# Loading four key heads at a time: 32 partitions per head, one 16 KB row per partition, weights turned on VectorE

## The chip, the cores and the metric

The kernel runs on 1 core of one Trainium2 chip. The metric is the time of one execution on the device, in microseconds (us); the kernel before takes 199.07 us (median of 3 runs, 198.92 to 199.16). A run that is more than 1.5% above the fastest of its kernel counts as slow and is left out of comparisons.

Words used below, as they apply to this kernel: TensorE does the matrix products and writes them to PSUM; VectorE and ScalarE copy from PSUM and do the work between the products; SyncE issues the loads. A *packet* is one record of the DMA in the trace, a run of contiguous bytes (8 KB of keys or values in the kernel before). The profile counts 16 DMA engines for the core. A *unit* is the work for 4 key heads of one batch entry; there are 16 units.

## The reference, cut to what matters

One decoding step: 8 batch entries with one token each, 16 query heads, 8 key heads of size 256, and only the last 1,024 of 4,096 cached positions. The result is mixed with a small MLP.

```python
# x (8, 1, 448); k_cache, v_cache (8, 8, 4096, 256), bf16; W = 1024; rep = 2
q = (x @ wq).reshape(B, 1, 16, 256).transpose(0, 2, 1, 3)
k = repeat(k_cache[:, :, Sk - W:, :], 2, axis=1)
v = repeat(v_cache[:, :, Sk - W:, :], 2, axis=1)
scores = einsum("bhqd,bhkd->bhqk", q, k) * 256 ** -0.5
p = softmax(scores)
a = einsum("bhqk,bhkd->bhqd", p, v)...reshape(B, 1, 4096) @ wo
out = g * a + (1 - g) * mlp(layernorm(x))      # g: a sigmoid gate per token
```

The keys and values that are needed are 8 x 8 x 1,024 x 256 x 2 bytes, twice: 67.1 MB. In memory, the 1,024 rows of one head are one contiguous block of 512 KB; the blocks of two heads lie 2 MB apart.

## The kernel before

A ring of 18 buffers of 1 MB is filled by loads from SyncE in the order of use. One load brings 2 heads; partition p holds 16 rows (8 KB) of one head. The pattern on the memory side `s a (c d)` names the 64 row groups first and the 2 heads second, so heads alternate from partition to partition.

```python
QUAD = 4; GP = 2; NCK = 16; SK = 64; SLOT = 4096; RING = 18      # cut

def kv_loader(src, b, g):
    def load(t):
        nc.sync.dma_start(
            t[:],
            src[b, g : g + GP, kv_base:Sk, :].rearrange(
                "a (s c) d -> s a (c d)", c=NCK
            ),
        )
    return load
```

In each unit TensorE turns the keys in 64 blocks of 128x128, VectorE and ScalarE copy them from PSUM, TensorE makes the scores, and the softmax follows. Because the heads alternate over the partitions, ScalarE writes every exponential twice; 16 matmuls then turn the weights, and VectorE multiplies the wrong head's half with zero.

```python
def scores(u):                                   # cut
    nc.tensor.matmul(                            # 2 columns of weights, every 2nd column of keys
        S_ps[32 * a : 32 * a + rep, hf * NMM : (hf + 1) * NMM],
        lhsT=qw[:, j, b, h0 : h0 + rep],
        rhs=KT[a // GP][:, j, hf * CMM : (hf + 1) * CMM, :, a % GP], ...)

def softmax(u):                                  # cut
    nc.vector.reduce_max(nmx[:], S_ps[:], axis=AXIS.X, negate=True)
    nc.scalar.activation(                        # 1,024 scores to 2,048 exponentials
        E[:].rearrange("p (k a) -> p k a", a=GP),
        S_ps[:].rearrange("p (k o) -> p k o", o=1).to_broadcast([P, W, GP]),
        ACT.Exp, bias=nmx[:], scale=1.0, accum_out=rowsum[:])

def weights(u):                                  # cut
    for c in range(NCK):                         # 16 matmuls turn the weights
        nc.tensor.matmul(sm[:, c, :], lhsT=E[:, c * P : (c + 1) * P], rhs=sel[:], ...)
    nc.vector.tensor_tensor(ET[:], sm[:, 0:NCK, :], own[:]..., op=ALU.mult)

for u in range(1, NQ - 2):                       # the order of a unit
    transpose_keys(u)
    values(u - 1, *weights(u - 1))
    scores(u)
    softmax(u)
```

Of the kernel before, what the change touches and what calls it, by code (L numbers as in the profile page):

```python
# [17 lines left out]
def kernel(  # L18
# [38 lines left out]
    GP = 2  # L57
    NCK = NC * GP
    SK = P // GP
    SLOT = 4096  # L60
# [4 lines left out]
    RING = 18  # L65
    NMM = 512
    CMM = NMM // SK
# [30 lines left out]
    def kv_loader(src, b, g):  # L98
        def load(t):
            nc.sync.dma_start(  # L100
                t[:],
                src[b, g : g + GP, kv_base:Sk, :].rearrange(
                    "a (s c) d -> s a (c d)", c=NCK
                ),
            )

        return load
# [22 lines left out]
    def add_kv(name, src, u):  # L130
        b, half = divmod(u, Hkv // QUAD)
        for s in range(2):
            add((name, u, s), kv_loader(src, b, half * QUAD + 2 * s))

    wq_m = A_wq[0:DM, :].rearrange("(p r) n -> p r n", r=NR)
# [5 lines left out]
    W2A = SLOT // D  # L141

    add_kv("k", A_k_cache, 0)
    add(("w1", 0), rows_loader([w1_m[:, 0 : 2 * F]]))
    add(("w1", 1), rows_loader([w1_m[:, 2 * F : 3 * F], w1_t]))
    for r in range(NR):
        add(("wq", r), rows_loader([wq_m[:, r, :]]))
    add(("wq", NR), rows_loader([wq_t]))
    add(("w2", 0), rows_loader([w2_v[:, 0 : W2A * D]]))
    add(("w2", 1), rows_loader([w2_v[:, W2A * D : NF * D]]))  # L150
# [7 lines left out]
    for q in range(NHQ):  # L158
        for j0, j1 in WO_PARTS[q]:
            add(("wo", q, j0), rows_loader([wo_v[:, q, j0 * D : j1 * D]]))  # L160

    def slot(*key):
        return slots[index[key]]
# [36 lines left out]
    sel = consts.tile([P, RQ], BF16)  # L200
    qw = consts.tile([P, NJ, NB, Hq], BF16)
# [18 lines left out]
    for h in range(2):  # L220
        nc.vector.tensor_copy(xz[:, h, h::2], x_sb[:, DM:D])
    transposed(xT, x_sb, xz)
    nc.vector.tensor_copy(
        sel[:].rearrange("p (a i) -> p a i", i=rep),
        ident[:].rearrange("p (a s) -> p a s", a=QUAD)[:, :, 0:rep],
    )

    par = consts.tile([P, GP], F32)
    own = consts.tile([P, RQ], F32)
    nc.vector.reduce_sum(  # L230
        par[:], ident[:].rearrange("p (s a) -> p a s", a=GP), axis=AXIS.X
    )
    nc.vector.tensor_copy(
        own[:].rearrange("p (t a i) -> p t a i", a=GP, i=rep),
        par[:]
        .rearrange("p (t a i) -> p t a i", t=1, i=1)
        .to_broadcast([P, QUAD // GP, GP, rep]),
    )
# [61 lines left out]
    def transpose_keys(u):  # L300
        for s in range(2):
            kn = slot("k", u, s)
            kt = ktpool.tile([P, NJ, NCK, SK, GP], BF16, tag="kt", name="kt")
            KT[s] = kt
            ktf = kt[:].rearrange("p j c s a -> p j (c s a)")
            for c0 in range(0, NCK, NC):
                for j in range(NJ):
                    ktp = ps_kt.tile([P, W], BF16, tag="ktp", name="ktp")
                    for c in range(NC):
                        o = (c0 + c) * Dh + j * P  # L310
                        nc.tensor.transpose(  # L311
                            ktp[:, c * P : (c + 1) * P], kn[:, o : o + P], ident[:]
                        )
                    dst = ktf[:, j, c0 * P : (c0 + NC) * P]
                    if evac[0] % 8 in (2, 4, 7):
                        nc.scalar.copy(dst, ktp[:])  # L316
                    else:
                        nc.vector.tensor_copy(dst, ktp[:])  # L318
                    evac[0] += 1
            done()  # L320

    def query():
        qt = ps_misc.tile([P, Hq * NJ, NB], F32, tag="misc", name="qt")
        for r in range(NR + 1):
            w = slot("wq", r)
            for k in range(Hq * NJ):
# [4 lines left out]
                    lhsT=w[:, c : c + P],  # L331
# [5 lines left out]
            done()  # L337
        for j in range(NJ):
            nc.vector.tensor_scalar_mul(  # L339
                qw[:, j, :, :],  # L340
                qt[:].rearrange("p (h j) b -> p j b h", j=NJ)[:, j],
                qscale,
            )

    def scores(u):
        b, half = divmod(u, Hkv // QUAD)
        for hf in range(W // NMM):
            for j in range(NJ):
                for a in range(QUAD):
                    h0 = (half * QUAD + a) * rep  # L350
                    nc.tensor.matmul(  # L351
                        S_ps[32 * a : 32 * a + rep, hf * NMM : (hf + 1) * NMM],
                        lhsT=qw[:, j, b, h0 : h0 + rep],
                        rhs=KT[a // GP][:, j, hf * CMM : (hf + 1) * CMM, :, a % GP],
# [6 lines left out]
    def softmax(u):  # L361
        nmx = epool.tile([P, 1], F32, tag="nmx", name="nmx")
        nc.vector.reduce_max(nmx[:], S_ps[:], axis=AXIS.X, negate=True)  # L363
        E = epool.tile([P, W * GP], BF16, tag="E", name="E")
        rowsum = epool.tile([P, 1], F32, tag="rowsum", name="rowsum")
        nc.scalar.activation(  # L366
            E[:].rearrange("p (k a) -> p k a", a=GP),
            S_ps[:].rearrange("p (k o) -> p k o", o=1).to_broadcast([P, W, GP]),
            ACT.Exp,
            bias=nmx[:],  # L370
            scale=1.0,
            accum_out=rowsum[:],
# [3 lines left out]
    def weights(u):  # L376
        E, rowsum = soft.pop(u)
        rsum = epool.tile([P, 1], F32, tag="rsum", name="rsum")
        nc.vector.reciprocal(rsum[:], rowsum[:])
        selr = epool.tile([P, RQ], F32, tag="selr", name="selr")  # L380
        nc.vector.tensor_scalar(  # L381
            selr[:], sel[:], rsum[:], float(GP), op0=ALU.mult, op1=ALU.mult
        )
        sm = ps_sm.tile([P, NCK + 1, RQ], F32, tag="sm", name="sm")
        for c in range(NCK):
# [207 lines left out]
```

## Time and profile before

| | before | where it is read |
|---|---|---|
| time | 199.07 us | runs |
| TensorE, VectorE, ScalarE busy | 75%, 48%, 42% | part 1 of the page |
| bytes read | 77.68 MB | part 3 |
| rate from 30 to 180 us | 417 GB/s | windows |
| row maximum to row maximum | 10.16 us in most units, 10.24 in the mean of 12 | times of the row maxima, 39.40 to 49.56 and 39.40 to 162.27 us |
| last output-weight piece lands | 193.44 us | chain of waits |

From the page of the kernel before: the span in 40 slices of 4.9 us. A digit is a tenth: for PEclk of the full TensorE clock, for DMA of the mean busy time of the 16 engines. Then the hardware queue (packets, MB, share of all 16 engines' time), the shares of the chain that ended last, and the loads (times issued, KB, us from issue to landing).

```profile
PEclk9996556999999996799999999999999999997555
DMA  4999999999999999999999999999999999999960
GB/s 170 416 427 406 420 412 414 421 414 424 411 414 419 419 419 416 414 419 419 423 411 411 423 416 423 409 418 423 416 416 413 418 419 419 421 411 416 413 246 23
...
q1 hardware_dynamic: 11424, 77.68, 95.8%
...
DMA 49%; PE 26%; DVE 16%; ACT 5%; issue 2%; SPq 0%; ACTq 0%
...
slot<-in_A_k_cache_dram SPq DMA_DIRECT2D x32, 1024.0 KB, 19.9
slot<-in_A_v_cache_dram SPq DMA_DIRECT2D x32, 1024.0 KB, 19.9
```

The DMA engines hardly rest between the start and the end (9 tenths or more in slices 2 to 38): loads set the time. The groups of instructions (line, engine, operation, shapes, count, then busy us and mean ns of one) show the parts that the change touches. `slot` is a buffer of the ring, `ktp` the turned keys in PSUM, `kt` their copy, `S_ps` the scores, `nmx` the row maximum, `E` the exponentials, `sm` and `ET` the turned weights, `po` the attention's outputs:

```profile
L311 PE MATMUL ktp<-ident,slot 128*128 128x128 bf16 x1024 | 73.9, 232 | 21.6 <-ACT kt L316 15.2
...
L366 ACT ACTIVATE E<-S_ps,nmx 128x2048 bf16<-128x2048 f32 x16 | 31.5, 1968 | 72.2 <-DVE nmx L363 72.2
...
L351 PE MATMUL S_ps<-kt,qw 128*2 128x512 bf16 x256 | 18.1, 402 | 0.4 <-DVE qw L339 0.4
...
L386 PE MATMUL sm<-sel,E 128*128 128x8 bf16 x256 | 8.8, 167 | 1.7 <-ACT E L366 1.7
```

The last column is the idle time just before, and what ended most of it. The key transposes waited 15.2 us in all for ScalarE's copies, which stand behind the exponential of 1.97 us.

### The profile page before, as it was taken

What the parts mean: (1) busy time and instruction counts of PE and PEld (TensorE: products, weight loads), DVE (VectorE), ACT (ScalarE), POOL (GpSimd) and SP (SyncE); (2) the same over time, 40 slices, a digit from 0 to 9 for tenths busy, and PEclk for the clock granted to TensorE, in tenths of its full rate; (3) what the DMA queues carried; (4) which work ended last, traced back from release to release, by engine and by line L of the source; (5) the groups of instructions that cost most, each with busy time, mean ns of one, the idle gap of its engine ahead of it and who ended that gap; (6) DMA issues with size and microseconds to landing.
All of it is one profiled execution on the core that took longest, in us unless ns stands there. A gap on an engine that the chain in (4) does not pass through costs nothing.

```text
span 197.0 us, 6578 instructions
## 1 busy us (share of the span) xinstructions
PE 147.7 (75%) x3006; PEld 125.1 (64%) x3006; DVE 94.3 (48%) x230; ACT 82.0 (42%) x85; POOL 0.9 (0%) x7
## 2 busy tenths in 40 slices
PE   1699869868686878979596868686868686887662
PEld 0699739656574758877575667575656665675641
DVE  6540335364646464555545454636363636763200
ACT  3250043272636354362718180808172727383000
POOL 1000000000000000000000000000000000000000
PEclk9996556999999996799999999999999999997555
DMA  4999999999999999999999999999999999999960
GB/s 170 416 427 406 420 412 414 421 414 424 411 414 419 419 419 416 414 419 419 423 411 411 423 416 423 409 418 423 416 416 413 418 419 419 421 411 416 413 246 23
DMA packets 11645, 78.10 MB, mean 396 GB/s; under 512 B 1489, under 2 KB 1890, under 8 KB 3042
## 3 DMA queue, kind: packets, MB, share of 16 engines
q1 hardware_dynamic: 11424, 77.68, 95.8%
q8 instruction: 23, 0.38, 0.8%
q10 hardware_dynamic: 194, 0.02, 0.1%
q14 instruction: 4, 0.03, 0.0%
HBM read 77.68 MB, written 0.01 MB: 394 GB/s over the span
## 4 chain that ended last, share of the span: by engine, by line
DMA 49%; PE 26%; DVE 16%; ACT 5%; issue 2%; SPq 0%; ACTq 0%
DMA slot<-in_A_v_cache_dram 31%; PE ktp L311 10%; DMA slot<-in_A_wq_dram 8%; DVE kt L318 7%; PE po L414 7%; DMA slot<-in_A_wo_dram 7%; DVE nmx L363 6%; PE S_ps L351 5%; ACT kt L316 4%; DMA slot<-in_A_k_cache_dram 3%; PE sm L393 2%; ACT E L366 1%; DVE ET L395 1%; DVE selr L381 1%; PE bb L484 1%
## 5 line engine op out<-in xcount | busy, mean ns | idle before, releaser
L311 PE MATMUL ktp<-ident,slot 128*128 128x128 bf16 x1024 | 73.9, 232 | 21.6 <-ACT kt L316 15.2
L311 PEld LDWEIGHTS <-slot 128*128 128x128 bf16 x1024 | 66.1, 105 | 33.3 <-issue 28.3
L318 DVE COPY kt<-ktp 128x1024 bf16<-128x1024 bf16 x80 | 52.5, 686 | 30.3 <-PE ktp L311 29.0
L366 ACT ACTIVATE E<-S_ps,nmx 128x2048 bf16<-128x2048 f32 x16 | 31.5, 1968 | 72.2 <-DVE nmx L363 72.2
L316 ACT COPY kt<-ktp 128x1024 bf16<-128x1024 bf16 x48 | 47.1, 1013 | 19.3 <-PE ktp L311 19.3
L414 PEld LDWEIGHTS <-slot 128*128 128x128 bf16 x1024 | 29.5, 99 | 6.8 <-issue 6.8
L414 PE MATMUL po<-ET,slot 128*128 128x4 bf16 x1024 | 28.1, 164 | 5.3 <-DVE ET L395 5.3
L363 DVE TENSOR_REDUCE nmx<-S_ps 128x1 f32<-128x1024 f32 x16 | 19.6, 1225 | 13.0 <-PE S_ps L351 13.0
L351 PE MATMUL S_ps<-kt,qw 128*2 128x512 bf16 x256 | 18.1, 402 | 0.4 <-DVE qw L339 0.4
L423 DVE TENSOR_TENSOR oT<-po,rb 128x8 bf16<-128x8 f32 x32 | 4.3, 190 | 26.5 <-PE po L414 26.5
L393 PE MATMUL sm<-selr,ones_f 128*128 128x8 f32 x32 | 6.6, 279 | 5.5 <-DVE selr L381 5.5
L386 PE MATMUL sm<-sel,E 128*128 128x8 bf16 x256 | 8.8, 167 | 1.7 <-ACT E L366 1.7
L393 PEld LDWEIGHTS sm<-selr,ones_f 128*128 128x128 f32 x32 | 5.2, 203 | 6.8 <-DVE selr L381 6.6
L386 PEld LDWEIGHTS <-E 128*128 128x128 bf16 x256 | 8.2, 97 | 1.8 <-ACT E L366 1.8
L395 DVE TENSOR_TENSOR ET<-sm,own 128x128 bf16<-128x128 f32 x16 | 4.7, 291 | 8.2 <-PE sm L393 8.2
L351 PEld LDWEIGHTS <-qw 128*2 128x2 bf16 x256 | 4.7, 82 | 5.2 <-DVE qw L339 0.5
L545 PE MATMUL A_ps<-slot,oP 128*8 128x112 bf16 x128 | 4.3, 290 | 2.8 <-DMA slot<-in_A_wo_dram 2.1
L545 PEld LDWEIGHTS <-oP 128*8 128x8 bf16 x128 | 2.9, 113 | 4.1 <-issue 3.4
L329 PE MATMUL qt<-xT,slot 128*128 128x8 bf16 x128 | 3.9, 168 | 0.8 <-DMA slot<-in_A_wq_dram 0.4
L329 PEld LDWEIGHTS <-slot 128*128 128x128 bf16 x128 | 3.7, 104 | 1.0 <-DMA slot<-in_A_wq_dram 0.6
L381 DVE TENSOR_SCALAR selr<-sel,rsum 128x8 f32<-128x8 bf16 x16 | 3.7, 231 | 0.6
L552 DVE SCALAR_TENSOR_TENSOR res<-A_ps,gg_s,mixb 128x112 bf16<-128x112 f32 x1 | 0.3, 335 | 6.6 <-PE A_ps L545 6.6
(69 smaller groups left out, 38.9 us busy)
## 6 DMA issues: line engine op xcount, KB each, us to landing
slot<-in_A_k_cache_dram SPq DMA_DIRECT2D x32, 1024.0 KB, 19.9
slot<-in_A_v_cache_dram SPq DMA_DIRECT2D x32, 1024.0 KB, 19.9
slot<-in_A_wq_dram SPq DMA_DIRECT2D x3, 1024.0 KB
slot<-in_A_wo_dram SPq DMA_DIRECT2D x3, 896.0 KB, 19.1
slot<-in_B_w_dram SPq DMA_DIRECT2D x1, 1008.0 KB
slot<-in_B_w_dram SPq DMA_DIRECT2D x1, 896.0 KB
slot<-in_B_w_dram SPq DMA_DIRECT2D x1, 560.0 KB
slot<-in_A_wq_dram SPq DMA_DIRECT2D x1, 512.0 KB
```

Of the source, the lines that this page charges most:

```text
L311: nc.tensor.transpose(ktp[:, c * P : (c + 1) * P], kn[:, o : o + P], ident[:])
L316: nc.scalar.copy(dst, ktp[:])
L318: nc.vector.tensor_copy(dst, ktp[:])
L329: nc.tensor.matmul(qt[:, k, :], lhsT=w[:, c : c + P], rhs=xT[:, r + half, :], start=(r == 0 and k == 0), stop=(r == NR), skip_group_check= ...
L351: nc.tensor.matmul(S_ps[32 * a : 32 * a + rep, hf * NMM : (hf + 1) * NMM], lhsT=qw[:, j, b, h0 : h0 + rep], rhs=KT[a // GP][:, j, hf * CMM ...
L363: nc.vector.reduce_max(nmx[:], S_ps[:], axis=AXIS.X, negate=True)
L366: nc.scalar.activation(E[:].rearrange("p (k a) -> p k a", a=GP), S_ps[:].rearrange("p (k o) -> p k o", o=1).to_broadcast([P, W, GP]), ACT.Exp,
L386: nc.tensor.matmul(sm[:, c, :], lhsT=E[:, c * P : (c + 1) * P], rhs=sel[:], start=True, stop=True,)
L393: nc.tensor.matmul(sm[:, NCK, :], lhsT=ones_f[:], rhs=selr[:], start=True, stop=True)
L395: nc.vector.tensor_tensor(ET[:], sm[:, 0:NCK, :], own[:].rearrange("p (o r) -> p o r", o=1).to_broadcast([P, NCK, RQ]), op=ALU.mult,)
L414: nc.tensor.matmul(PO[:, j, cols], lhsT=vn[:, o : (c + 1) * Dh : NJ], rhs=ET[:, c, cols], start=(c == 0), stop=(c == NCK - 1),)
L545: nc.tensor.matmul(dst, lhsT=oP[:, j, q, :], rhs=w[:, o + cols.start : o + cols.stop], start=(q == 0 and j == 0), stop=(q == NHQ - 1 and j ...
```

## The change

The intent: longer runs for the DMA engines (16 KB instead of 8 KB), one load for four heads, and less compute. Each head gets its own 32 partitions. The exponentials are then needed once only, and a VectorE transpose, which the program counts on to turn blocks of 32x32, puts the weights where the values need them. The weights that TensorE holds for the scores are 8 columns wide, 6 of them zero; the rows of foreign heads get a maximum so low that their exponentials are zero. The diff, cut to its core:

```diff
-    NCK = NC * GP          # 16
-    SK = P // GP           # 64
-    SLOT = 4096
-    RING = 18
+    SK = P // QUAD         # 32
+    NCK = W // SK          # 32
+    SLOT = 8192
+    RING = 9
@@ loads @@
-    def kv_loader(src, b, g):
-        def load(t):
-            nc.sync.dma_start(
-                t[:],
-                src[b, g : g + GP, kv_base:Sk, :].rearrange(
-                    "a (s c) d -> s a (c d)", c=NCK
-                ),
-            )
+    def kv_loader(src, u, parts):
+        b, half = divmod(u, Hkv // QUAD)
+        v = src[b, half * QUAD : (half + 1) * QUAD, kv_base:Sk, :].rearrange(
+            "a (s c) d -> a s (c d)", c=NCK
+        )
+        def load(t):
+            n = NCK * Dh // parts
+            for i in range(parts):
+                nc.sync.dma_start(
+                    t[:, i * n : (i + 1) * n], v[:, :, i * n : (i + 1) * n]
+                )
@@ scores @@
-                        S_ps[32 * a : 32 * a + rep, hf * NMM : (hf + 1) * NMM],
-                        lhsT=qw[:, j, b, h0 : h0 + rep],
-                        rhs=KT[a // GP][:, j, hf * CMM : (hf + 1) * CMM, :, a % GP],
+                        S_ps[32 * a : 32 * a + RQ, hf * CH * SK : (hf + 1) * CH * SK],
+                        lhsT=qw[:, j, b, half, a, :],
+                        rhs=KT[hf][:, j, :, a * SK : (a + 1) * SK],
@@ softmax and weights @@
+        nc.vector.tensor_tensor(nmx[:], nmx[:], cap[:], op=ALU.min)
-            E[:].rearrange("p (k a) -> p k a", a=GP),
-            S_ps[:].rearrange("p (k o) -> p k o", o=1).to_broadcast([P, W, GP]),
-            ACT.Exp, ...
+            E[:], S_ps[:], ACT.Exp, bias=nmx[:], scale=1.0, accum_out=rowsum[:]
-        for c in range(NCK):
-            nc.tensor.matmul(sm[:, c, :], lhsT=E[:, c * P : (c + 1) * P], rhs=sel[:], ...)
-        nc.vector.tensor_tensor(ET[:], sm[:, 0:NCK, :], own[:]..., op=ALU.mult)
+        nc.vector.transpose(ET[:].rearrange("p c r -> p (c r)"), E[:])
[... value loads and weight loads: one buffer where there were two; the rest is bookkeeping ...]
```

In the loader, `s a` has become `a s`: the memory side now names the 4 heads first, which gives each head its own 32 partitions.

More of the change, by code (lines that the diff above doesn't have):

```diff
@@ L56 @@
     NQ = NB * Hkv // QUAD
-    GP = 2
-    NCK = NC * GP
-    SK = P // GP
-    SLOT = 4096
+    SK = P // QUAD
+    NCK = W // SK
+    NH = 2
+    CH = NCK // NH
+    SLOT = 8192
     HPQ = 4
@@ L64 @@
     WO_PARTS = [[(0, NJ8)]] * (NHQ - 1) + [[(0, 4), (4, 6), (6, 8)]]
-    RING = 18
-    NMM = 512
-    CMM = NMM // SK
+    RING = 9
+    BIG = 1e30
     qscale = float(Dh) ** -0.5
@@ L128, in add, with add_kv @@
         plan.append(loader)
-    def add_kv(name, src, u):
-        b, half = divmod(u, Hkv // QUAD)
-        for s in range(2):
-            add((name, u, s), kv_loader(src, b, half * QUAD + 2 * s))
-    wq_m = A_wq[0:DM, :].rearrange("(p r) n -> p r n", r=NR)
+    def add_kv(name, src, u, parts=1):
+        add((name, u), kv_loader(src, u, parts))
+    wq_m = A_wq[0:DM, :].rearrange("(p r) n -> p (r n)", r=NR)
     wq_t = A_wq[DM:D, :].rearrange("r (h n) -> (r h) n", h=2)
@@ L140 @@
     wo_v = A_wo.rearrange("(q p j) n -> p q (j n)", p=P, j=NJ8)
-    W2A = SLOT // D
-    add_kv("k", A_k_cache, 0)
-    add(("w1", 0), rows_loader([w1_m[:, 0 : 2 * F]]))
-    add(("w1", 1), rows_loader([w1_m[:, 2 * F : 3 * F], w1_t]))
-    for r in range(NR):
-        add(("wq", r), rows_loader([wq_m[:, r, :]]))
-    add(("wq", NR), rows_loader([wq_t]))
-    add(("w2", 0), rows_loader([w2_v[:, 0 : W2A * D]]))
-    add(("w2", 1), rows_loader([w2_v[:, W2A * D : NF * D]]))
+    add_kv("k", A_k_cache, 0, parts=2)
+    add(("w1",), rows_loader([w1_m, w1_t]))
+    add(("wq", 0), rows_loader([wq_m[:, 0 : 2 * HD]]))
+    add(("wq", 1), rows_loader([wq_m[:, 2 * HD : 3 * HD], wq_t]))
+    add(("w2",), rows_loader([w2_v]))
     for u in range(1, NQ - 1):
@@ L157 @@
         add_kv("v", A_v_cache, u)
-    for q in range(NHQ):
-        for j0, j1 in WO_PARTS[q]:
-            add(("wo", q, j0), rows_loader([wo_v[:, q, j0 * D : j1 * D]]))
+    for q in range(0, NHQ, 2):
+        add(
+            ("wo", q),
+            rows_loader(
+                [
+                    wo_v[:, q + i, j0 * D : j1 * D]
+                    for i in range(2)
+                    for j0, j1 in WO_PARTS[q + i]
+                ]
+            ),
+        )
     def slot(*key):
@@ L199 @@
     yT = consts.tile([P, NX, NB], BF16)
-    sel = consts.tile([P, RQ], BF16)
-    qw = consts.tile([P, NJ, NB, Hq], BF16)
+    sel = consts.tile([P, RQ], F32)
+    qw = consts.tile([P, NJ, NB, Hq // RQ, QUAD, RQ], BF16)
     oT = consts.tile([P, Hq, NJ, NB], BF16)
@@ L222 @@
     transposed(xT, x_sb, xz)
-    nc.vector.tensor_copy(
-        sel[:].rearrange("p (a i) -> p a i", i=rep),
-        ident[:].rearrange("p (a s) -> p a s", a=QUAD)[:, :, 0:rep],
-    )
-    par = consts.tile([P, GP], F32)
-    own = consts.tile([P, RQ], F32)
-    nc.vector.reduce_sum(
-        par[:], ident[:].rearrange("p (s a) -> p a s", a=GP), axis=AXIS.X
-    )
-    nc.vector.tensor_copy(
-        own[:].rearrange("p (t a i) -> p t a i", a=GP, i=rep),
-        par[:]
-        .rearrange("p (t a i) -> p t a i", t=1, i=1)
-        .to_broadcast([P, QUAD // GP, GP, rep]),
-    )
+    nc.vector.reduce_sum(
+        sel[:], ident[:].rearrange("p (a s) -> p s a", a=QUAD)[:, 0:RQ, :], axis=AXIS.X
+    )
+    cap = consts.tile([P, 1], F32)
+    rows = consts.tile([P, 1], F32)
+    for a in range(QUAD):
+        nc.vector.reduce_sum(
+            rows[32 * a : 32 * a + 32, :],
+            ident[32 * a : 32 * a + 32, (32 + rep) * a : (32 + rep) * a + rep],
+            axis=AXIS.X,
+        )
+    nc.vector.tensor_scalar(
+        cap[:], rows[:], 2.0 * BIG, -BIG, op0=ALU.mult, op1=ALU.add
+    )
+    nc.vector.memset(qw[:], 0.0)
     def norm_and_gate():
@@ L300, in transpose_keys @@
     def transpose_keys(u):
-        for s in range(2):
-            kn = slot("k", u, s)
-            kt = ktpool.tile([P, NJ, NCK, SK, GP], BF16, tag="kt", name="kt")
-            KT[s] = kt
-            ktf = kt[:].rearrange("p j c s a -> p j (c s a)")
-            for c0 in range(0, NCK, NC):
+        kn = slot("k", u)
+        for hf in range(NH):
+            kt = ktpool.tile([P, NJ, CH, P], BF16, tag="kt", name="kt")
+            KT[hf] = kt
+            for c0 in range(0, CH, NC):
                 for j in range(NJ):
-                    ktp = ps_kt.tile([P, W], BF16, tag="ktp", name="ktp")
+                    ktp = ps_kt.tile([P, NC, P], BF16, tag="ktp", name="ktp")
                     for c in range(NC):
-                        o = (c0 + c) * Dh + j * P
-                        nc.tensor.transpose(
-                            ktp[:, c * P : (c + 1) * P], kn[:, o : o + P], ident[:]
-                        )
-                    dst = ktf[:, j, c0 * P : (c0 + NC) * P]
+                        o = (hf * CH + c0 + c) * Dh + j * P
+                        nc.tensor.transpose(ktp[:, c, :], kn[:, o : o + P], ident[:])
+                    dst = kt[:, j, c0 : c0 + NC, :]
                     if evac[0] % 8 in (2, 4, 7):
@@ L319, in transpose_keys @@
                     evac[0] += 1
-            done()
+        done()
     def query():
@@ L324, in query @@
         for r in range(NR + 1):
-            w = slot("wq", r)
+            w, o = slot("wq", r // 2), (r % 2) * HD
             for k in range(Hq * NJ):
@@ L330, in query @@
                     qt[:, k, :],
-                    lhsT=w[:, c : c + P],
+                    lhsT=w[:, o + c : o + c + P],
                     rhs=xT[:, r + half, :],
@@ L336, in query @@
                 )
-            done()
-        for j in range(NJ):
-            nc.vector.tensor_scalar_mul(
-                qw[:, j, :, :],
-                qt[:].rearrange("p (h j) b -> p j b h", j=NJ)[:, j],
-                qscale,
-            )
+        done(2)
+        qv = qt[:].rearrange("p (g a i j) b -> p a j b g i", g=Hq // RQ, a=QUAD, i=rep)
+        for a in range(QUAD):
+            for j in range(NJ):
+                nc.vector.tensor_scalar_mul(
+                    qw[:, j, :, :, a, a * rep : (a + 1) * rep], qv[:, a, j], qscale
+                )
     def scores(u):
         b, half = divmod(u, Hkv // QUAD)
-        for hf in range(W // NMM):
+        for hf in range(NH):
             for j in range(NJ):
                 for a in range(QUAD):
-                    h0 = (half * QUAD + a) * rep
                     nc.tensor.matmul(
-                        S_ps[32 * a : 32 * a + rep, hf * NMM : (hf + 1) * NMM],
-                        lhsT=qw[:, j, b, h0 : h0 + rep],
-                        rhs=KT[a // GP][:, j, hf * CMM : (hf + 1) * CMM, :, a % GP],
+                        S_ps[32 * a : 32 * a + RQ, hf * CH * SK : (hf + 1) * CH * SK],
+                        lhsT=qw[:, j, b, half, a, :],
+                        rhs=KT[hf][:, j, :, a * SK : (a + 1) * SK],
                         start=(j == 0),
@@ L363, in softmax @@
         nc.vector.reduce_max(nmx[:], S_ps[:], axis=AXIS.X, negate=True)
-        E = epool.tile([P, W * GP], BF16, tag="E", name="E")
+        nc.vector.tensor_tensor(nmx[:], nmx[:], cap[:], op=ALU.min)
+        E = epool.tile([P, W], BF16, tag="E", name="E")
         rowsum = epool.tile([P, 1], F32, tag="rowsum", name="rowsum")
         nc.scalar.activation(
-            E[:].rearrange("p (k a) -> p k a", a=GP),
-            S_ps[:].rearrange("p (k o) -> p k o", o=1).to_broadcast([P, W, GP]),
-            ACT.Exp,
-            bias=nmx[:],
-            scale=1.0,
-            accum_out=rowsum[:],
+            E[:], S_ps[:], ACT.Exp, bias=nmx[:], scale=1.0, accum_out=rowsum[:]
         )
@@ L377, in weights @@
         E, rowsum = soft.pop(u)
-        rsum = epool.tile([P, 1], F32, tag="rsum", name="rsum")
-        nc.vector.reciprocal(rsum[:], rowsum[:])
         selr = epool.tile([P, RQ], F32, tag="selr", name="selr")
-        nc.vector.tensor_scalar(
-            selr[:], sel[:], rsum[:], float(GP), op0=ALU.mult, op1=ALU.mult
-        )
-        sm = ps_sm.tile([P, NCK + 1, RQ], F32, tag="sm", name="sm")
-        for c in range(NCK):
-            nc.tensor.matmul(
-                sm[:, c, :],
-                lhsT=E[:, c * P : (c + 1) * P],
-                rhs=sel[:],
-                start=True,
-                stop=True,
-            )
-        nc.tensor.matmul(sm[:, NCK, :], lhsT=ones_f[:], rhs=selr[:], start=True, stop=True)
-        ET = epool.tile([P, NCK, RQ], BF16, tag="ET", name="ET")
-        nc.vector.tensor_tensor(
-            ET[:],
-            sm[:, 0:NCK, :],
-            own[:].rearrange("p (o r) -> p o r", o=1).to_broadcast([P, NCK, RQ]),
-            op=ALU.mult,
-        )
+        nc.vector.tensor_scalar_mul(selr[:], sel[:], rowsum[:])
+        sm = ps_sm.tile([P, RQ], F32, tag="sm", name="sm")
+        nc.tensor.matmul(sm[:], lhsT=ones_f[:], rhs=selr[:], start=True, stop=True)
+        ET = epool.tile([P, NCK, 32], BF16, tag="ET", name="ET")
+        nc.vector.transpose(ET[:].rearrange("p c r -> p (c r)"), E[:])
         rb = epool.tile([P, RQ], F32, tag="rb", name="rb")
-        nc.vector.tensor_copy(rb[:], sm[:, NCK, :])
+        nc.vector.reciprocal(rb[:], sm[:])
         return ET, rb
@@ L407, in values @@
         PO = ps_po.tile([P, NJ, RQ], F32, tag="po", name="po")
-        for s in range(2):
-            vn = slot("v", u, s)
-            cols = slice(GP * rep * s, GP * rep * (s + 1))
-            for j in range(NJ):
-                for c in range(NCK):
-                    o = c * Dh + j
-                    nc.tensor.matmul(
-                        PO[:, j, cols],
-                        lhsT=vn[:, o : (c + 1) * Dh : NJ],
-                        rhs=ET[:, c, cols],
-                        start=(c == 0),
-                        stop=(c == NCK - 1),
-                    )
-            done()
-        for j in range(NJ):
-            nc.vector.tensor_tensor(
-                oT[:, half * RQ : (half + 1) * RQ, j, b],
-                PO[:, j, :],
-                rb[:],
-                op=ALU.mult,
-            )
+        vn = slot("v", u)
+        for j in range(NJ):
+            for c in range(NCK):
+                nc.tensor.matmul(
+                    PO[:, j, :],
+                    lhsT=vn[:, c * Dh + j : (c + 1) * Dh : NJ],
+                    rhs=ET[:, c, 0:RQ],
+                    start=(c == 0),
+                    stop=(c == NCK - 1),
+                )
+        done()
+        nc.vector.tensor_tensor(
+            oT[:, half * RQ : (half + 1) * RQ, :, b].rearrange("p h j -> p j h"),
+            PO[:],
+            rb[:].rearrange("p (o r) -> p o r", o=1).to_broadcast([P, NJ, RQ]),
+            op=ALU.mult,
+        )
     def mlp_hidden():
         hT = ps_misc.tile([P, NF, NB], F32, tag="misc", name="hT")
-        w1a, w1b = slot("w1", 0), slot("w1", 1)
+        w = slot("w1")
         for r in range(NR):
-            w, o = (w1a, r * F) if r < 2 else (w1b, 0)
+            o = r * F
             for c in range(NF):
@@ L447, in mlp_hidden @@
                     hT[64 * h : 64 * h + 64, c, :],
-                    lhsT=w1b[:, F + c : F + FH : NF],
+                    lhsT=w[:, NR * F + c : NR * F + FH : NF],
                     rhs=yT[:, NR + h, :],
@@ L453, in mlp_hidden @@
                 )
-        done(2)
+        done()
         z = consts.tile([P, NF, NB], F32)
@@ L481, in mlp_out @@
         for c in range(NF):
-            w, o = (slot("w2", 0), c) if c < W2A else (slot("w2", 1), c - W2A)
+            w = slot("w2")
             for dst, cols in quads(bb):
@@ L486, in mlp_out @@
                     lhsT=hs[:, c, :],
-                    rhs=w[:, o * D + cols.start : o * D + cols.stop],
+                    rhs=w[:, c * D + cols.start : c * D + cols.stop],
                     start=(c == 0),
@@ L494, in mlp_out @@
             )
-        done(2)
+        done()
         nc.vector.tensor_scalar_mul(mixb[:], bb[:], gg_s[:, 1:2])
@@ L539 @@
     for q in range(NHQ):
-        for j0, j1 in WO_PARTS[q]:
-            w = slot("wo", q, j0)
-            for j in range(j0, j1):
-                for dst, cols in quads(A_ps):
-                    o = (j - j0) * D
-                    nc.tensor.matmul(
-                        dst,
-                        lhsT=oP[:, j, q, :],
-                        rhs=w[:, o + cols.start : o + cols.stop],
-                        start=(q == 0 and j == 0),
-                        stop=(q == NHQ - 1 and j == NJ8 - 1),
-                    )
+        w = slot("wo", q - q % 2)
+        for j in range(NJ8):
+            o = ((q % 2) * NJ8 + j) * D
+            for dst, cols in quads(A_ps):
+                nc.tensor.matmul(
+                    dst,
+                    lhsT=oP[:, j, q, :],
+                    rhs=w[:, o + cols.start : o + cols.stop],
+                    start=(q == 0 and j == 0),
+                    stop=(q == NHQ - 1 and j == NJ8 - 1),
+                )
     nc.vector.scalar_tensor_tensor(
```

## The prediction

> **What bounds it now.** DMA. The page's 40 slices show the 16 DMA engines at 9 tenths or more from 5 to 183 us, 410 to 427 GB/s, 77.68 MB read; TensorE is busy 75%, VectorE 48%, ScalarE 42%. The chain of waits from 118 us on is DMA alone (three value loads, then the output weights, last landing 193.44 us), then 0.4 us of matmul, 0.34 us of VectorE and the output DMA. From 29 to 118 us it runs through compute, 10.16 us from one row maximum to the next, against 9.97 us between key loads at the queue: a near second limit, absorbed by the ring. The DMA share falls to one half from 188.5 to 191 us: half of the engines end some 4 us late[...]. That half sets the end.
>
> **DMA.** The trace's packet records give the time of one packet: 1,792 bytes 74 ns, 3,584 140, 7,168 272, 8,192 309 to 313: a line with about 7 ns per packet. [...] Of 536 packets of 8 KB per engine, 524 become 262 of 16 KB, estimated at 611 to 619 ns. Saved per engine: 262 x 7 to 8 ns = 1.9 us, at most 4 us if the excess over the line goes too. Some 35 fewer completion packets (9 ns) give 0.3 us, longer weight rows 0.1 us. Sum about 2.4 us, all critical. 512 fewer TensorE instructions mean two instruction packets fewer[...]: nothing from that.
>
> **Compute, per unit of 4 heads (16 of them).**
> - ScalarE: the exponential handles 1,024 instead of 2,048 elements: 1.97 us to about 1.05. Its key copies come 0.9 us sooner; these held TensorE 15.2 us in all.
> - TensorE: 16 matmuls (0.55 us) removed.
> - VectorE: reciprocal, multiply and one output multiply go (0.15, 0.29, 0.19); a block transpose of 128x1024 comes. [...] I estimate 1.2 us, like the 1,024-element maximum (1.225 us). No run shows it yet. The cap adds about 0.1.
> - Compute chain: -0.9, +0.3 (transpose for matmul and multiply), +0.1: 10.16 to about 9.6 us. Worth nothing by itself, but DMA stays the limit at 9.85 us a unit.
>
> **Ring and tail.** 9 slots of 2 MB hold what 18 of 1 MB did; a late release still leaves 7 x 2 MB queued. The last output-weight pieces keep sizes and waits: the tail stays 3.6 us.
>
> **Prediction.** 199.07 - 2.5 = 196.5 us, 8 in 10 within 195.2 to 198.1. Faster by over 2% 0.10, within 2% 0.88, slower 0.02.
>
> **What would show it.** 16 KB packets of 611 to 619 ns; 421 to 426 GB/s in the middle against 417; last output-weight landing near 191; exponential near 1.05 us, transpose near 1.2 us; row maxima at the period of the loads; key transposes waiting on DMA instead of ScalarE; the half-share tail still there.
>
> **What would make it wrong.** 16 KB runs at other HBM addresses slower, or clearly faster, than the line; a transpose of twice my estimate[...].

Passages that no trace or run of this case shows are cut from the prediction, here and in the expectations below. 1.9 us from longer packets, 0.3 from fewer 4-byte packets of 9 ns (the "completion packets": 1,288 in the kernel before, 348 in the changed one) and 0.1 from longer weight rows were put at about 2.4 us, taken off as 2.5 to give 196.5 us. The instruction packets (23 before, 21 after) added nothing to it; what is measured of the tail is the DMA share, 0.55 from 188.5 to 191 us. The transpose's 1.2 us is an estimate from the 1.225 us of the row maximum over as many elements. It is part of the 9.6 us of a unit, not of the 2.4 us.

## The result, and the profile after

The changed kernel takes 697.79 us (median of 4 runs, 692.23 to 705.66, one of them counted as slow). It takes 3.50 times as long: the ratio of fast runs is 3.4964, 95% interval 3.4637 to 3.5291. Ratios here are the mean time of one kernel's fast runs over that of the other's fast runs of the same rounds, so not quite the ratio of the medians. The output of the changed kernel is right.

From the page of the changed kernel, the same lines as before (slices are now 17.5 us):

```profile
PEclk9955555556555565556555565556555565665555
DMA  8932222222222222222222222222222222225521
GB/s 163 212 116 86 88 103 109 108 107 108 107 109 107 108 109 106 110 106 106 103 109 107 108 108 107 109 106 109 98 108 107 108 109 106 110 107 162 155 114 52
...
q1 hardware_dynamic: 6132, 77.67, 30.1%
...
another core or an unknown queue 61%; PE 19%; DMA 11%; SPq 4%; DVE 3%; issue 1%; ACT 0%; ACTq 0%
...
L315 PE MATMUL ktp<-ident,slot 128*128 128x128 bf16 x1024 | 95.4, 279 | 274.9 <-DMA slot<-in_A_k_cache_dram 273.3
...
L368 ACT ACTIVATE E<-S_ps,nmx 128x1024 bf16<-128x1024 f32 x16 | 17.8, 1113 | 264.7 <-DVE nmx L365 264.7
...
L380 DVE STREAM_TRANSPOSE ET<-E 128x1024 bf16<-128x1024 bf16 x16 | 19.8, 1237 | 0.0
```

The bytes are the same, yet the DMA digit falls from 9 to 2, and the key transposes wait 273.3 us for their loads. The chain cannot name what it waits for in most of the time ("another core or an unknown queue"), so it is of no help here; the DMA row is. A view of a window in the middle gives the numbers; its columns are the window, its length, busy us of TensorE, weight loads, VectorE, ScalarE and GpSimd, the granted clock, the DMA share and GB/s:

```profile
100.00:600.00 500.00, 123.00 (x1832) 98.89 (x1832) 77.79 (x135) 51.99 (x62) 0.00 (x0) 0.56 0.25 107
```

A share of 0.25 is what 4 of 16 engines give. The trace's packet records say the same without an average. For each kernel below, 200 moments between 40% and 80% of the trace were taken, and the packets of 8 KB or more under way at each were counted:

| kernel | outermost size on the memory side | packets under way, mean | median ns of one | GB/s in the middle |
|---|---|---|---|---|
| before (8 KB) | 64 | 16.2 | 313 | 417 |
| changed (16 KB) | 4 | 4.06 | 614 | 107 |

So each packet is as fast as it was predicted to be, 614 ns, but only four run at a time. (The packet records do not name the engine. Numbers of engines in this document are read from the packets under way and from the DMA share.) The changed kernel has 4,096 packets of 16 KB; on 4 engines that is 1,024 each, and 1,024 x 614 ns = 629 us of the 692 to 706.

### The profile page after: what moved, and what is told of

Read it like the earlier page. It is cut to its first block, busy times and chain, and to the rows that moved or that the text cites. A ratio compares the mean times of both kernels' runs of the same rounds, so it can differ in the third digit from the quotient of the medians.

```text
span 700.1 us, 6010 instructions
## 1 busy us (share of the span) xinstructions
PE 177.4 (25%) x2750; PEld 146.1 (21%) x2750; DVE 111.1 (16%) x224; ACT 71.1 (10%) x85; POOL 0.8 (0%) x7
## 4 chain that ended last, share of the span: by engine, by line
another core or an unknown queue 61%; PE 19%; DMA 11%; SPq 4%; DVE 3%; issue 1%; ACT 0%; ACTq 0%
PE ktp L315 10%; DMA slot<-in_A_wq_dram 6%; DMA slot<-in_A_wo_dram 5%; PE S_ps L352 4%; SPq L123 4%; PE po L391 4%; DVE kt L320 3%; PE sm L378 1%; DVE selr L376 0%; ACT kt L318 0%; PE bb L459 0%; DVE nmx L364 0%; SPq L107 0%; PE qt L331 0%
## 5 line engine op out<-in xcount | busy, mean ns | idle before, releaser
L315 PE MATMUL ktp<-ident,slot 128*128 128x128 bf16 x1024 | 95.4, 279 | 274.9 <-DMA slot<-in_A_k_cache_dram 273.3
L315 PEld LDWEIGHTS <-slot 128*128 128x128 bf16 x1024 | 90.9, 131 | 289.4 <-DMA slot<-in_A_k_cache_dram 286.3
L391 PE MATMUL po<-ET,slot 128*128 128x8 bf16 x1024 | 29.9, 168 | 223.7 <-DMA slot<-in_A_v_cache_dram 223.7
L391 PEld LDWEIGHTS <-slot 128*128 128x128 bf16 x1024 | 28.5, 104 | 225.9 <-DMA slot<-in_A_v_cache_dram 225.9
L368 ACT ACTIVATE E<-S_ps,nmx 128x1024 bf16<-128x1024 f32 x16 | 17.8, 1113 | 264.7 <-DVE nmx L365 264.7
L399 DVE TENSOR_TENSOR oT<-po,rb 128x16 bf16<-128x16 f32 x16 | 3.6, 225 | 241.1 <-PE po L391 241.1
L352 PE MATMUL S_ps<-kt,qw 128*8 128x512 bf16 x256 | 29.8, 606 | 0.3 <-DVE qw L343 0.3
L380 DVE STREAM_TRANSPOSE ET<-E 128x1024 bf16<-128x1024 bf16 x16 | 19.8, 1237 | 0.0
L352 PEld LDWEIGHTS <-qw 128*8 128x8 bf16 x256 | 6.7, 104 | 9.3 <-issue 7.9
L331 PEld LDWEIGHTS <-slot 128*128 128x128 bf16 x128 | 3.7, 104 | 0.8 <-DMA slot<-in_A_wq_dram 0.3
L376 DVE TENSOR_SCALAR selr<-sel,rowsum 128x8 f32<-128x8 f32 x16 | 3.5, 218 | 0.0
L368 ACT ACTIVATION_READ_ACCUMULATOR E<-S_ps,nmx 128x1 f32 x16 | 3.1, 193 | 0.0
```

Source lines behind the costliest of these rows:

```text
L315: nc.tensor.transpose(ktp[:, c, :], kn[:, o : o + P], ident[:])
L331: nc.tensor.matmul(qt[:, k, :], lhsT=w[:, o + c : o + c + P], rhs=xT[:, r + half, :], start=(r == 0 and k == 0), stop=(r == NR), skip_grou ...
L352: nc.tensor.matmul(S_ps[32 * a : 32 * a + RQ, hf * CH * SK : (hf + 1) * CH * SK], lhsT=qw[:, j, b, half, a, :], rhs=KT[hf][:, j, :, a * SK ...
L368: nc.scalar.activation(E[:], S_ps[:], ACT.Exp, bias=nmx[:], scale=1.0, accum_out=rowsum[:])
L380: nc.vector.transpose(ET[:].rearrange("p c r -> p (c r)"), E[:])
L391: nc.tensor.matmul(PO[:, j, :], lhsT=vn[:, c * Dh + j : (c + 1) * Dh : NJ], rhs=ET[:, c, 0:RQ], start=(c == 0), stop=(c == NCK - 1),)
```

## The experiments

Theory A: a load is spread over no more DMA engines than the outermost dimension of its memory side has entries, if that is under 16. It is a theory that fits the table: 64 row groups with 16.2 packets under way, 4 heads with 4.06; the SBUF side has 128 partitions in both. Rival B: the 16 KB runs, or four heads that lie 2 MB apart, are slow for the memory.

A word on right values. Some experiments put heads on the wrong partitions. They still passed the comparison with the reference on the chip, since with this data the softmax is nearly flat and the attention hardly shows in the output. In a functional simulation with enlarged keys, queries and values, where the attention made 0.88 of the output, the run with row groups first was off by more than the largest output itself, while the kernel before, the changed one, the load per head and the three permuted versions were all within 0.0035 of the largest output. That simulation says nothing of the chip's transposes, and nothing of time.

### Row groups first

```diff
-            "a (s c) d -> a s (c d)", c=NCK
+            "a (s c) d -> s a (c d)", c=NCK
```

> One word pattern changed in the changed kernel: the HBM side of each key and value load names the 32 row groups first and the 4 heads second, as the kernel before did with its 64 and 2; same 16 KB runs, same addresses, same bytes. The values come out wrong on purpose (heads land on other partitions). Theory A (a load is spread over no more DMA engines than its outermost HBM dimension has entries, 4 in the changed kernel): all 16 engines work again, over 410 GB/s, 196.5 us as predicted, range 195 to 199. Rival B (16 KB runs at 2 MB head pitch are slow for HBM): still near 690 us.

Measured: 199.18 us (198.94 to 199.73, 4 runs), ratio to the kernel before 0.9985 (0.991 to 1.006). One exchange of two letters, with the same runs and the same addresses, takes 500 us away: rival B falls. On average 16.1 packets are under way, of 614 ns in the median. But the time is just outside what theory A expected, and nothing of the predicted gain is left, although the rate is 424 GB/s. From its page:

```profile
PEclk9999555899579957996699997599859985999555
DMA  4999999999999999999999999999999999999710
GB/s 164 416 431 405 444 422 415 424 427 430 427 427 424 424 420 424 424 427 420 420 425 420 440 424 427 424 427 424 424 422 424 424 424 424 420 423 408 302 49 3
...
PE 44%; DVE 27%; DMA 15%; issue 6%; ACT 5%; ACTq 0%
```

The loads are done earlier (the DMA row falls off a slice sooner), and the chain that ended last is now compute: TensorE 44%, VectorE 27%. The row maxima lie at 103.99, 113.69 and 124.29 us; these are the two units, in the columns of the window view:

```profile
103.99:113.69 9.70, 7.27 (x148) 5.97 (x147) 6.16 (x12) 4.04 (x5) 0.00 (x0) 1.00 1.00 424
113.69:124.29 10.60, 8.17 (x148) 6.13 (x147) 6.16 (x11) 4.03 (x5) 0.00 (x0) 0.86 1.02 431
```

With the full clock a unit takes 9.70 us, with the clock at half for a part of it 10.60. From 42.14 to 165.50 us there are 12 units: 10.28 us each, while a unit's 4.19 MB need 9.89 us at 424 GB/s. This is theory C: with all engines on, compute is the limit.

### Two, four, eight and sixteen engines

Two more points of the series. In the first, a load takes 16 rows of all 8 heads instead of 32 rows of 4 heads; in the second, the kernel before gets the order `a s`. Both give wrong values.

```diff
-        v = src[b, half * QUAD : (half + 1) * QUAD, kv_base:Sk, :].rearrange(
-            "a (s c) d -> a s (c d)", c=NCK
-        )
+        v = src[b, :, kv_base:Sk, :].rearrange("a (s c) d -> a s (c d)", c=NCK)[
+            :, half * 16 : half * 16 + 16
+        ]
```

> The changed kernel, each load taking 16 rows of 16 KB of all 8 heads instead of 32 rows of 4 heads: outermost dimension 8, same bytes in all. Values wrong on purpose. Theory A: 8 engines, about 213 GB/s in the middle, DMA share one half, time 335 to 365 us. Rival B: near 690 us, as the runs and the pitch between heads are the same.

Measured: 422.79 us, one run. The window from 200 to 380 us:

```profile
200.00:380.00 180.00, 86.67 (x1226) 71.04 (x1227) 54.52 (x93) 36.15 (x43) 0.00 (x0) 0.61 0.54 212
```

8.1 packets are under way on average. The rate and the share are what theory A expected; the whole is 58 us above its range, because before that window some slices reached only 129 to 154 GB/s at a share of about one half, with packets longer than 614 ns, and the last three slices only 78, 53 and 22 GB/s. Why is open in both cases.

```diff
-                    "a (s c) d -> s a (c d)", c=NCK        # in the kernel before
+                    "a (s c) d -> a s (c d)", c=NCK
```

> The kernel before with its 8 KB runs, the heads named first (2, then 64 rows) in each key and value load. Values wrong on purpose. Theory A: 2 engines, about 53 GB/s in the middle, DMA share one eighth, time 1270 to 1340 us. Rival B (the 16 KB runs are at fault): stays near 199 us.

Measured: 1,325.67 us, one run; 2.04 packets under way, and from 200 to 1,200 us:

```profile
200.00:1200.00 1000.00, 149.84 (x2042) 124.90 (x2042) 72.71 (x154) 66.24 (x65) 0.00 (x0) 0.53 0.13 53
```

So the order alone ruins the kernel before as well, with 8 KB runs. Sizes 2, 4, 8 and 32 give 2, 4, 8 and 16 engines and 53, 107, 212 and 424 GB/s: the number of engines that theory A gives holds in every case.

### One load per head

The obvious repair that keeps the layout: four loads of 32 rows each.

```diff
-                nc.sync.dma_start(
-                    t[:, i * n : (i + 1) * n], v[:, :, i * n : (i + 1) * n]
-                )
+                for a in range(QUAD):
+                    nc.sync.dma_start(
+                        t[32 * a : 32 * a + 32, i * n : (i + 1) * n],
+                        v[a, :, i * n : (i + 1) * n],
+                    )
```

> The changed kernel with each load cut into four, one per head: 32 rows of 16 KB onto 32 partitions, outermost dimension 32. Correct values. Theory A: 16 engines again, so far faster than 690 us. How fast is open: [...]. Rival B (16 KB runs and head pitch): near 690 us.

Measured: 348.03 us (346.76 to 351.26), ratio 1.7479 (1.7338 to 1.7621). From its page:

```profile
DMA  8999999999999999999999999999999999999991
GB/s 179 336 406 296 208 212 212 207 197 214 210 212 212 216 218 216 214 221 216 213 214 220 224 216 220 216 218 220 214 223 222 216 227 227 235 235 245 226 329 68
```

This row is a trap: all 16 engines are busy (a share of 1.01 from 60 to 320 us), and move half of what they could, 219 GB/s there against 424 with row groups first. A 16 KB packet now takes 1,226 ns in the median instead of 614. What differs from that run is that one load covers one head and 32 partitions, not four and 128. The trace shows the factor of two, not its cause.

### Other queues

Two edits of one line each, with right values: values from ScalarE's queue, or both from GpSimd.

```diff
-                nc.sync.dma_start(
+                (nc.sync if src is A_k_cache else nc.scalar).dma_start(      # two queues
+                nc.gpsimd.dma_start(                                         # GpSimd
```

> The changed kernel as it is, keys issued from SyncE's queue and values from ScalarE's. Theory A[...] the DMA share stays a quarter and the time 690 us or more (ScalarE may wait in its issues). Rival E (a limit of each queue, or of how fast one queue hands out rows): the share doubles and the time falls to 350 to 400 us.

Measured: 760.13 us, one run; 4.05 packets under way, about 2 of each queue. So a second queue adds no engines: the two together have no more packets under way than the one had (4.06), at the same share of 0.25:

```profile
250.00:600.00 350.00, 82.00 (x1184) 65.36 (x1176) 53.15 (x90) 33.93 (x40) 0.00 (x0) 0.55 0.25 104
```

> The changed kernel as it is, its key and value loads issued from GpSimd instead of SyncE. Right values. [...] theory A then expects loads in flight on different engines, DMA share over nine tenths, and 200 to 230 us. If GpSimd's queue uses the same 4 engines always[...], 690 us or more.

Measured: 657.28 us, one run, and neither case of the expectation. On average 15.9 packets are under way, so all engines work, but one packet of 16 KB takes 2,187 ns:

```profile
100.00:500.00 400.00, 104.25 (x1630) 87.39 (x1622) 70.32 (x122) 46.62 (x56) 14.77 (x22) 0.58 1.02 118
```

Loads from GpSimd do reach more engines (a share of 1.02 against 0.25), and it does not help here (118 GB/s against 107). Why the packets are 3.6 times as long was not looked into.

### Why the gain was missing with 16 engines: the clock

Two runs ask why TensorE's clock falls in about every second unit. In the traces it is full or half, for multiples of 3.41 us (in the kernel before from 3.41 to 95.57 us). With row groups first it is mostly four steps at full and two at half, 20.5 us together, about two units. TensorE hardly waits for loads in that run (2.2 us in all before the key transposes). The guess was another wait: TensorE waits 0.76 us for the VectorE transpose in each unit of that run, where the kernel before waited 0.38 us. No run shows that idleness halves the clock. To test the guess, one run puts the 16 matmuls that the change had removed ahead of that wait (nothing reads them), and one makes the score matmuls 2 columns wide again. Both give wrong values, as the run they start from.

```diff
+        for c in range(16):                                    # filler
+            nc.tensor.matmul(sm[:, c, :], lhsT=E[:, (c % NC) * P : (c % NC + 1) * P],
+                             rhs=ident[:, 0:RQ], start=True, stop=True)
```

> The run with row groups first, plus 16 matmuls per unit that nothing reads, ahead of the wait for the transposed weights (the 16 that the change had removed, on the same weights). Values wrong on purpose, as there. Theory C1 (the clock falls because TensorE idles in that wait): granted clock from 0.81 back to about 0.9, unit 9.7 us nearly always, time 196 to 197.5 us. Rival C2 (the clock falls for another reason, such as more work at once): clock 0.81 or lower, time 199 us or more.

Measured: 199.15 us (199.11 to 199.22), clock 0.814 against 0.815 without the filler. But the filler did not fill the wait that it was meant for. The group of the value matmuls, first without and then with the filler:

```profile
L391 PE MATMUL po<-ET,slot 128*128 128x8 bf16 x1024 | 28.6, 167 | 11.3 <-DVE ET L380 9.8
L401 PE MATMUL po<-ET,slot 128*128 128x8 bf16 x1024 | 28.5, 167 | 10.1 <-DVE ET L390 9.7
```

TensorE waited for the transposed weights (`ET`) as long as before, still 0.76 us in a unit. The filler ran before the matmul that adds up the row sums, and shortened the wait in front of that one, from 7.0 to 1.7 us over the run. So this earlier wait is not the cause; whether the wait for the transpose is one was not tested.

```diff
-                        S_ps[32 * a : 32 * a + RQ, hf * CH * SK : (hf + 1) * CH * SK],
-                        lhsT=qw[:, j, b, half, a, :],
+                        S_ps[32 * a : 32 * a + rep, hf * CH * SK : (hf + 1) * CH * SK],
+                        lhsT=qw[:, j, b, half, a, a * rep : (a + 1) * rep],
```

> The run with row groups first in its first order, the score matmuls 2 weight columns wide instead of 8 (no zero rows computed; the rows keep their zeros from the start). Values wrong on purpose. Theory G (the wider score matmuls make TensorE's clock fall): granted clock from 0.81 to about 0.9, time 196 to 197.5 us. Rival H (the clock falls by how the waits of a unit of 9.7 us lie, not by the width): clock 0.8 to 0.83, time 199 us.

Measured: 199.22 us (198.73 to 199.36), clock 0.804. The width is not the cause. What makes the clock fall more often than in the kernel before stays open (0.85 against 0.97 in the middle of the two profiled runs; over whole fast runs of one job 0.799 to 0.815 against 0.815 to 0.880).

### Taking compute off the chain

If compute is the limit, a better order should give the loads their gain. This run does the scores of a unit ahead of the values of the last, so that the VectorE transpose runs beside the score matmuls, and the row maximum beside the value matmuls.

```diff
         transpose_keys(u)
-        values(u - 1, *weights(u - 1))
+        W0 = weights(u - 1)
         scores(u)
         softmax(u)
+        values(u - 1, *W0)
```

> The run with row groups first (16 engines, values wrong on purpose), and in each unit the scores of this unit ahead of the values of the last, so that the VectorE transpose runs beside the score matmuls and the row maximum beside the value matmuls. Theory C (compute at 10.3 us a unit, not DMA, held that run at 199.18 us): the unit falls to 8.2 us at full clock and some 9.2 at worst, under the 9.85 us of the loads; the queue becomes the limit and the prediction's sum for DMA alone is measured: 195.5 to 197 us, key transposes waiting on key loads. Rival D (the end is set by something that both runs share, such as late output weights or the slow half of the engines): 198.5 to 200 us.

Measured: 197.29 us (196.84 to 198.78, 6 runs), ratio 0.9922 (0.9871 to 0.9973). The chain that ended last is loads from 81 to 162 us, then compute in the last 29 us; its shares were PE 44% and DMA 15% before the reordering:

```profile
DMA 77%; PE 14%; DVE 5%; issue 2%; SPq 0%
```

The median lies just above the range of theory C (195.5 to 197), and two of the six runs, 198.39 and 198.78 us, lie in that of rival D. But the run with narrow scores, which keeps the first order, had 199.22 us in the median in the same job. So theory C holds in the main: with the same loads, another order of the same work gives 1.9 us, although the mean clock is no better (0.810).

### A version with right values

Row groups first puts heads on every fourth partition. To compute rightly there, the score matmuls take every fourth column of the turned keys, and the turned weights have to be brought into the same partition order, which one TensorE matmul with a permutation and a copy do.

```diff
-                        rhs=KT[hf][:, j, :, a * SK : (a + 1) * SK],
+                        rhs=KT[hf][:, j, :, a::QUAD],
...
+        nc.tensor.matmul(
+            sm[:, 0:NCK, :], lhsT=perm[:], rhs=ET[:, :, 0:RQ], start=True, stop=True
+        )
+        nc.vector.tensor_copy(EP[:], sm[:, 0:NCK, :])
```

> A version meant to be right and fast: loads with the 32 row groups first (16 engines, 16 KB runs, heads on every fourth partition); the score matmuls take every fourth column of the turned keys, and the turned weights are put into the same partition order by one TensorE matmul with a permutation and a VectorE copy per unit. Theory C (with 16 engines on, compute is the limit, and TensorE's clock falls to half in about every second unit): the added matmul and copy lie on the compute chain and cost 0.6 to 0.9 us a unit, so 205 to 214 us. Rival D (DMA still sets the time and the 199.18 us of the uncut test has another cause): 198 to 200 us.

Measured: 220.27 us (219.5 to 220.51), ratio 1.1062 (1.1044 to 1.1081). Compute is the limit as expected, and more so: the time is above the range of 205 to 214. Next, the better order, with the copy of the permuted weights on ScalarE ahead of the exponential:

```diff
         transpose_keys(u)
-        values(u - 1, *weights(u - 1))
+        W0 = weights(u - 1)
         scores(u)
+        W0 = permuted(*W0)
         softmax(u)
+        values(u - 1, *W0)
```

> The same with another order in each unit: after the key transposes come the scores of this unit, then the permutation of the last unit's weights, then its values; the copy of the permuted weights goes to ScalarE ahead of the exponential. Thus the VectorE transpose runs beside the score matmuls, and the row maximum beside the value matmuls. Theory C: the unit takes 8.8 to 9.4 us at full clock, compute leaves the chain, and the time is the prediction's sum for DMA alone: 195.5 to 197.5 us, last output-weight landing near 191 us. Rival D: 199 us as before the reordering.

Measured: 199.32 us (198.4 to 200.4, 6 runs), ratio 1.0023 (0.9995 to 1.0052): a miss for theory C as it stood. The group of the score matmuls tells why, one matmul being 628 ns in the mean where the run with row groups first had 485:

```profile
L358 PE MATMUL S_ps<-kt,qw 128*8 128x512 bf16 x256 | 32.4, 628 | 0.3 <-DVE qw L349 0.3
```

In the timeline, 16 of them took 1.98 us. Theory F: it is the stride of four, the reading of every fourth column only. The last version removes the stride by turning the keys against a permuted identity, which lets them come out head by head. No cost of that shows: a key transpose took 257 ns in the mean at a clock of 0.821, and 256 against the plain identity at 0.810, in the reordered run with row groups first:

```diff
-                        nc.tensor.transpose(ktp[:, c, :], kn[:, o : o + P], ident[:])
+                        nc.tensor.transpose(ktp[:, c, :], kn[:, o : o + P], turn[:])
...
-                        rhs=KT[hf][:, j, :, a::QUAD],
+                        rhs=KT[hf][:, j, :, a * SK : (a + 1) * SK],
```

> The reordered version with right values, with one more thing: the key transposes use a permuted identity, so that the turned keys come out head by head and the score matmuls read 32 columns in a row, not every fourth. Theory F (the stride is what makes 16 score matmuls take 1.9 us instead of 1.04): back to 1.04 us, unit 8.5 us at full clock, DMA the limit, 195.7 to 197.2 us, faster than before by 1 per cent or a little more. Rival (the score time comes from TensorE's clock): scores stay near 1.9 us, time near 199 us.

Measured: 196.97 us (196.85 to 197.21, 4 runs), against 199.02 us for the kernel before in the same job; ratio 0.9886 (0.9839 to 0.9934). It beats both kernels, by 1.1% over the kernel before. Its slowest run (197.21 us) is faster than every run of the kernel before in that job (198.76 and more). Its score matmuls, the DMA and clock rows, and the shares of its chain:

```profile
PEclk9999555799669979788887979696969985999558
DMA  4999999999999999999999999999999999999940
GB/s 168 420 434 401 446 420 418 420 430 420 423 427 417 430 427 430 423 420 423 427 428 423 430 420 430 423 430 427 412 427 420 427 423 427 423 423 411 399 177 3
...
DMA 96%; SPq 1%; issue 0%; DVE 0%; PE 0%
...
L364 PE MATMUL S_ps<-kt,qw 128*8 128x512 bf16 x256 | 18.0, 394 | 0.3 <-DVE qw L355 0.3
```

The score matmuls are back at 394 ns, at a lower mean clock (0.821) than in the version with the stride (0.864). The trace also lets one sort them by the clock at their start: in both versions 240 of the 256 started at full clock, and these took 629 ns in the median with the stride and 379 without. So it was the stride, not the clock, and theory F holds. (Every second column, as the kernel before reads them, cost next to nothing: 387 ns in the median.) The loads set the time again, with 12 units in 117.67 us (row maxima at 39.64 and 157.31 us), 9.81 us each. The end of the chain in order of time, with start and length in us:

```profile
171.79 18.89 DMA slot<-in_A_wo_dram
190.68 0.04 issue
190.73 0.30 PE A_ps L546 x8
191.02 0.02 issue
191.05 0.33 DVE res L553
```

## Why the prediction was wrong

196.5 us with a range of 195.2 to 198.1 was predicted, 697.79 us was measured.

**The step that failed** is in the part on DMA: "Of 536 packets of 8 KB per engine, 524 become 262 of 16 KB". It takes for granted that the packets stay spread over 16 engines. In the changed kernel no more than about four packets are under way (4.06), as if four engines shared the 4,096, 1,024 each, and the other twelve had none of them. Nothing in the profile of before could show it, for it does not follow from sizes or durations. What it follows from was at hand in the diff, where the memory side went from `s a` (64 outermost) to `a s` (4 outermost). The list of what would make the prediction wrong named slow runs at other addresses, not fewer engines. One sign that it named, key transposes that wait on DMA and not on ScalarE, did come (273.3 us), but from the missing engines and not from faster compute. Rows first instead of heads first gave 500 us back.

**The second step that failed** hides behind the first: "10.16 to about 9.6 us. Worth nothing by itself, but DMA stays the limit at 9.85 us a unit." At full clock the unit did take 9.70 us. On average it took 10.28, against 10.24 in the kernel before over the same 12 units: the clock was at half in parts of it (9.70 and 10.60 us in the two windows above), and in the mean the work removed bought nothing. So with 16 engines on, compute was the limit and the time was 199.18 us. Two possible causes of the clock, the width of the score matmuls and the wait before the row sums, were tested and fell. The wait for the transpose was not tested, and the cause is open. That compute held the time is shown by the two reordered runs.

**What was right**, point by point. The kernel before is limited by its loads: the version with right values shows that faster loads shorten the time once compute allows it. Packets of 16 KB: 611 to 619 ns predicted, 614 measured. The rate in the middle: 421 to 426 GB/s predicted, 424 with 16 engines. The last output weights: near 191 us predicted, 190.68 in the best version, where the half-share tail is still there (a DMA share of 0.54 from 186 to 188 us). The VectorE transpose: 1.2 us estimated, like the row maximum over as many elements (1.225), 1.24 measured. The exponential: 1.05 us predicted, 1.11 measured. The gain from DMA alone, 2.4 us predicted: the best version gains 2.05 us between the medians, with one more matmul and one more copy in each unit.

## What to carry to other kernels

When a load's pattern changes, count the DMA engines before the bytes: look at the size of the outermost dimension on the memory side (here 32 and 64 had 16 packets under way, 2, 4 and 8 as many as their size), and read the DMA row, which fell to a quarter (0.25) with 4 of 16 engines at work. A full DMA row is no proof either, as the load per head shows (a share of 1.01 at 219 GB/s): divide the bytes by the time, and look at the time of one packet. When one limit is near another, as compute at 10.16 us was to loads at 9.97 (the loads that the ring holds ahead hid the difference), a gain on one side is worth nothing until the other has moved away too.
